# A fused decaying-attention and token-mixer kernel: first batch's v scaled on VectorE, another order of loads and constants, states from two partial sums, mixer pieces spread, tail split over two engines

## The chip, the cores and the metric

One Trainium2 chip, one of its cores. The metric is device time in microseconds of one execution. TensorE (PE in the rows, PEld its weight loads), VectorE (DVE), ScalarE (ACT), GpSimd (POOL) and SyncE (SP) each run their own queue in the order in which the program wrote it.

## What is computed

Linear attention with a decay per head over 4 batches, 8 heads, 768 positions and head width 64, and then a token mixer without a softmax on the attention's output, all given in float32:

```
# attention, head by head, in blocks of positions
intra = (q k^T * lam^(i-j), i >= j) v
inter = (q * lam^(i+1)) state
state = lam^block * state + (k * lam^(block-1-j))^T v
# mixer; x is the attention's output, heads side by side [4, 768, 512]
wq, wk = x @ w_q, x @ w_k                      # [768, 64] each
mixed  = (wq @ wk^T / 8) @ x                   # no softmax
out    = relu(mixed) @ w_out                   # [4, 768, 512]
```

## The kernel before

The work unit is a pair: one batch b and two heads, so 4 pairs per batch (kk = 0 to 3) and 16 in all (n = 0 to 15). The 768 positions are cut into six chunks of 128; the two heads of a pair sit on the two halves of the 128 partitions. The decay is folded into the operands: v is divided by a power of lam (scale_v, L169, tile vn, with the table DvI), and q is multiplied by one when it has been transposed (qT, with the tables Dq). Then the state before chunk c is a plain sum of k^T v over the chunks ahead of it.

For each pair: load casts q, k and v to bf16 by three DMAs issued from GpSimd's queue (L72, L78: fq, fk, fv); scale_v multiplies v by DvI, for pair 0 on VectorE and for all others on GpSimd; turn (L187) transposes q and k on TensorE into trq and trk, which VectorE (qT) and ScalarE (kT) bring to SBUF; states (L219) sums k^T v into the five states at once (dps), and one VectorE cast copies them out (gs, L235); scores (L238) makes k q^T and VectorE masks it in four pieces (pr, L260); inter (L264) and values (L281) add the two products into oa, which ScalarE copies to xT (L300); flip (L308) transposes xT back, and VectorE copies it to xnat.

The mixer of a batch runs inside the pairs of the next batch: mix_pq and mix_pk in kk = 0 (projections, qkT and wkn), mix_py in kk = 1 (Y), mix_pm in kk = 2 (eight products pm, each with a ReLU on ScalarE into rmT, L374), and mix_po for each of six chunks (po, copied to osb by ScalarE, L392, and stored by SyncE). The line with done (L428) says in which pair which of the six po run. The last batch's mixer is a tail behind the loop.

The order of all work is the order in which the loop writes it: there is no scheduler (manual_schedule). In turn n of the loop TensorE gets scores(n), mixer pieces, flip(n-1), inter(n), values(n), states(n+1), turn(n+2). All PSUM tiles are taken in turn from one pool of eight buffers, so a tile waits for the tile eight places earlier to be copied out. GpSimd's queue carries all loads and 15 of the 16 scalings in one line; in the loop load(n+5) stands ahead of scale_v(n+2):

```
    for n in range(N):
        if n + AHEAD < N:
            load(n + AHEAD)
        ...
        if n + 2 < N:
            scale_v(n + 2)
```

Names: trq, trk, sc, dps, oa, xp, pq, pk, py, pm and po are PSUM tiles; wqk and wo hold the mixer's weights; E48, ET, ident, maskc, swap, lnl and lncol are constants of the start.

## Time and profile before

| | us |
|---|---|
| median of 3 runs (119.08 to 119.41) | 119.2 |
| the profiled execution | 119.18 |
| its span, first to last instruction | 117.5 |
| TensorE busy | 90.8 (77%) |
| GpSimd busy | 71.0 (60%) |
| ScalarE busy | 67.6 (58%) |
| VectorE busy | 60.2 (51%) |

The sum of the prediction is made against the profiled execution, 119.18 us, of which 1.7 us lie outside the span; it stands within 0.02 us of the median. A busy share is a mean over stages that have different limits: GpSimd's work ends some 80 us into the span, the mixer starts only with the second batch, and the tail has no loads and hardly any VectorE work.

### The profile page before, as it was taken

To read this page: it belongs to the slowest core of one execution; us is meant where nothing else is said; L and a number is where in the kernel's file an instruction comes from. 1 tells how busy PE (TensorE), PEld (TensorE's weight loads), DVE (VectorE), ACT (ScalarE), POOL (GpSimd) and SP (SyncE) were. 2 spreads that over 40 slices of the span, in tenths; PEclk is the share of its full clock that TensorE was granted. 3 is DMA by queue.
4 is the path that set the end of the run, shared out by engine and by line. 5 is a ranking of instruction groups with operands and counts; after the bars stand their busy time and mean duration, and the time that the engine had idled before them with its cause. 6 is when DMAs were issued, how large, how long until landed. Compare 5 with 4: busy or idle time off the path is not lost. (4 is left out here: it accounts for less than half of the span.)

```text
span 117.5 us, 3292 instructions
## 1 busy us (share of the span) xinstructions
PE 90.8 (77%) x1380; PEld 60.1 (51%) x1392; DVE 60.2 (51%) x124; ACT 67.6 (58%) x123; POOL 71.0 (60%) x74
## 2 busy tenths in 40 slices
PE   0046992009988999799999988999999898976960
PEld 0046681008867757384858646575766463621420
DVE  1716874004896698555746892938398371110000
ACT  4409553002344638985666599585839957449750
POOL 5994799999999999999999996240000000000000
PEclk9999999555799999999999999999999999999998
DMA  1999999999999999999999999570400025140283
GB/s 29 188 210 162 143 86 147 162 157 161 163 189 165 169 160 144 160 148 192 241 231 164 267 168 165 103 268 0 179 6 0 6 89 206 62 169 15 93 310 132
DMA packets 67934, 17.06 MB, mean 145 GB/s; under 512 B 64336, under 2 KB 64848, under 8 KB 67920
## 3 DMA queue, kind: packets, MB, share of 16 engines
q0 software_dynamic: 61216, 9.77, 112.2%
q1 hardware_dynamic: 6704, 7.08, 17.9%
q8 instruction: 11, 0.18, 0.6%
q14 instruction: 3, 0.02, 0.1%
HBM read 20.32 MB, written 6.29 MB: 226 GB/s over the span
## 5 line engine op out<-in xcount | busy, mean ns | idle before, releaser
L260 DVE TENSOR_TENSOR pr<-sc,maskc 128x384 bf16<-128x384 f32 x64 | 31.2, 550 | 1.0 <-PE sc L248 1.0
L179 POOL TENSOR_TENSOR vn<-fv,DvI 128x768 bf16<-128x768 bf16 x15 | 22.6, 1510 | 7.2 <-PE oa L292 3.9
L384 PE MATMUL po<-wo,rmT 128*128 128x512 bf16 x87 | 23.0, 380 | 3.2 <-ACT rmT L374 2.8
L235 DVE CAST gs<-dps 128x320 bf16<-128x320 f32 x16 | 7.9, 492 | 30.0 <-PE dps L226 30.0
L213 ACT COPY kT<-trk 128x768 bf16<-128x768 bf16 x16 | 12.8, 798 | 16.7 <-PE trk L209 16.7
L300 ACT CAST xT<-oa 128x384 bf16<-128x384 f32 x32 | 17.2, 592 | 6.8 <-PE oa L292 6.0
L392 ACT COPY osb<-po 128x512 f32<-128x512 f32 x24 | 14.1, 585 | 9.3 <-PE po L384 7.0
L384 PEld LDWEIGHTS <-rmT 128*128 128x128 bf16 x96 | 9.0, 98 | 13.9 <-ACT rmT L374 5.9
L78 POOL DMA_DIRECT2D fv<-in_v_dram x15 | 15.7, 1049 | 0.0
L78 POOL DMA_DIRECT2D fk<-in_k_dram x15 | 15.6, 1041 | 0.0
L226 PE MATMUL dps<-vn,fk 128*64 128x320 bf16 (+4 forms) x150 | 9.2, 254 | 7.9 <-POOL vn L179 7.9
L194 PE MATMUL trq<-ident,fq 128*64 128x128 bf16 x192 | 9.3, 237 | 7.5 <-DMA fq<-in_q_dram 7.5
L72 POOL DMA_DIRECT2D fq<-in_q_dram x16 | 14.4, 898 | 0.8 <-POOLq L468 0.8
L374 ACT ACTIVATE rmT<-pm 128x384 bf16<-128x384 f32 x32 | 12.7, 530 | 0.4 <-PE pm L367 0.4
L226 PEld LDWEIGHTS <-fk 128*64 128x64 bf16 x150 | 7.9, 113 | 8.7 <-issue 8.2
L292 PE MATMUL oa<-pr,vn 128*64 128x128 bf16 x192 | 10.3, 228 | 1.1 <-DVE pr L260 0.7
L194 PEld LDWEIGHTS <-fq 128*64 128x64 bf16 x192 | 6.9, 121 | 7.5 <-DMA fq<-in_q_dram 7.5
L313 DVE COPY xnat<-xp 128x768 bf16<-128x768 bf16 x16 | 8.8, 550 | 3.5 <-PE xp L312 3.5
L312 PE MATMUL xp<-ident,xT 128*128 128x128 bf16 x96 | 8.6, 226 | 0.6 <-ACT xT L300 0.5
L200 DVE TENSOR_TENSOR qT<-trq,dq 128x768 bf16<-128x768 bf16 x16 | 8.8, 550 | 0.4 <-PE trq L194 0.4
L248 PE MATMUL sc<-qT,kT 64*128 64x128 bf16 x192 | 8.8, 229 | 0.0
L292 PEld LDWEIGHTS <-vn 128*64 128x64 bf16 x192 | 6.7, 112 | 3.7 <-issue 2.1
(45 smaller groups left out, 95.7 us busy)
## 6 DMA issues: line engine op xcount, KB each, us to landing
out_dram<-osb SPq DMA_DIRECT2D x24, 256.0 KB, 2.0
fq<-in_q_dram POOLq DMA_DIRECT2D x16, 192.0 KB, 5.9
fk<-in_k_dram POOLq DMA_DIRECT2D x15, 192.0 KB, 6.4
fv<-in_v_dram POOLq DMA_DIRECT2D x15, 192.0 KB, 6.7
wo<-in_moe_w_out_dram POOLq DMA_DIRECT2D x1, 512.0 KB, 7.3
k<-in_k_dram SPq DMA_DIRECT2D x1, 384.0 KB, 4.0
v<-in_v_dram SPq DMA_DIRECT2D x1, 384.0 KB, 7.1
wqk<-in_moe_w_q_dram POOLq DMA_DIRECT2D x2, 64.0 KB, 5.3
```

The lines of the kernel that those rows point to most:

```text
L72: nc.gpsimd.dma_start(out=t, in_=q_rows(n))
L78: nc.gpsimd.dma_start(out=t, in_=kv_rows(n, src))
L179: eng.tensor_tensor(out=vn, in0=fv, in1=DvI[:, 2 * kk : 2 * kk + 2, :].unsqueeze(3).to_broadcast([128, 2, NCH, D]), op=ALU.mult,)
L194: nc.tensor.transpose(trq[hl * 64 : hl * 64 + 64, a, r, :], fq[:, hl, a, r * D : (r + 1) * D], ident,)
L213: nc.scalar.copy(out=kT, in_=trk)
L226: nc.tensor.matmul(dps[hl * 64 : hl * 64 + 64, c:, :], kn[:, hl, c, :], vn[:, hl, c, :].unsqueeze(1).to_broadcast([128, m, D]), start=(c = ...
L260: nc.vector.tensor_tensor(out=t, in0=sc[a, hl], in1=maskc, op=ALU.mult)
L292: nc.tensor.matmul(oa[a][r, cc, :], vn[:, hl, c, :], pr[a, hl][:, cc, :], start=False, stop=(cc == 2), skip_group_check=True,)
L300: nc.scalar.copy(out=xT[b][:, kk, a * HALF : (a + 1) * HALF].rearrange("d (c p r) -> d c r p", c=3, r=2), in_=oa[a].rearrange("d c (r p) - ...
L374: nc.scalar.activation(out=M[b]["rmT"][:, dd, n * HALF : (n + 1) * HALF], in_=pm, func=ACT.Relu, scale=1.0 / 8.0,)
L384: nc.tensor.matmul(po, M[b]["rmT"][:, kt, t * CH : (t + 1) * CH], wo[:, kt, :], start=(kt == 0), stop=(kt == 3),)
L392: nc.scalar.copy(out=osb, in_=po)
```

## The change

v of pair 0 is loaded as the other v are, from GpSimd's queue in bf16 and right behind the first q, and no longer by SyncE in float32. The scalings of pairs 1 to 3 move from GpSimd to VectorE; GpSimd scales from pair 4 on. load(1), load(2), load(3) and load(4) now follow one another with only constants between them, and the three casting loads of the mixer's projection weights on GpSimd become two float32 loads on SyncE and three casts on ScalarE in the loop's second turn, together with the two copies that make swap. states multiplies chunks 0 and 1 into the first two states only, and chunks 2 to 4 into the last three; VectorE then copies the second state aside (two), casts the first two, and adds two to the last three. mix_pm is cut in halves, one behind turn in kk = 1 and one in kk = 2; three po stand in kk = 2 and three in kk = 3. Behind the loop flip stands later, one more po is there, and the tail's copies of Y, its ReLUs and its output copies alternate between ScalarE and VectorE.

```diff
     load_q(0)
+    t0 = stage.tile([128, 2, NCH, D], BF16, tag="fv", name="fv")
+    nc.gpsimd.dma_start(out=t0, in_=kv_rows(0, v))
+    staged[0, "v"] = t0
...
-    v0 = consts.tile([128, 2, NCH, D], F32, name="v0")
-    nc.sync.dma_start(out=v0, in_=kv_rows(0, v))
+    wqk_f = consts.tile([128, 2, 4, DHY], F32, name="wqk_f")
+    for i, w in enumerate((moe_w_q, moe_w_k)):
+        nc.sync.dma_start(out=wqk_f[:, i], in_=w.rearrange("(kt p) j -> p kt j", p=128))
...
-    def load_wqk():
-        for at, w in ((0, moe_w_q), (1, moe_w_k), (2, moe_w_q)):
-            nc.gpsimd.dma_start(
-                out=wqk[:, :, at * DHY : (at + 1) * DHY],
-                in_=w.rearrange("(kt p) j -> p kt j", p=128),
-            )
+    def cast_wqk():
+        nc.scalar.copy(out=wqk[:, :, 0:DHY], in_=wqk_f[:, 0])
+        nc.scalar.copy(out=wqk[:, :, DHY : 2 * DHY], in_=wqk_f[:, 1])
+        nc.scalar.copy(out=wqk[:, :, 2 * DHY :], in_=wqk_f[:, 0])
+        nc.vector.tensor_copy(out=swap[:, 0:64], in_=ident[:, 64:128])
+        nc.vector.tensor_copy(out=swap[:, 64:128], in_=ident[:, 0:64])
...
         for c in range(NCH - 1):
-            m = NCH - 1 - c
+            end = 2 if c < 2 else NCH - 1
             for hl in range(2):
                 nc.tensor.matmul(
-                    dps[hl * 64 : hl * 64 + 64, c:, :],
+                    dps[hl * 64 : hl * 64 + 64, c:end, :],
                     kn[:, hl, c, :],
-                    vn[:, hl, c, :].unsqueeze(1).to_broadcast([128, m, D]),
+                    vn[:, hl, c, :].unsqueeze(1).to_broadcast([128, end - c, D]),
...
-        nc.vector.tensor_copy(out=gs, in_=dps)
+        two = gsp.tile([128, 1, D], F32, tag="two", name="two")
+        nc.vector.tensor_copy(out=two, in_=dps[:, 1:2, :])
+        nc.vector.tensor_copy(out=gs[:, 0:2, :], in_=dps[:, 0:2, :])
+        nc.vector.tensor_tensor(
+            out=gs[:, 2:, :],
+            in0=dps[:, 2:, :],
+            in1=two.to_broadcast([128, NCH - 3, D]),
+            op=ALU.add,
+        )
...
+        if last:
+            nc.vector.tensor_copy(out=Y[:, 0:256], in_=py[:, 0:256])
+            nc.scalar.copy(out=Y[:, 256:], in_=py[:, 256:])
...
+                if last and dd % 2:
+                    nc.vector.tensor_scalar(
+                        out=to,
+                        in0=pms[dd, n],
...
+        if last and t % 2:
+            nc.vector.tensor_copy(out=osb, in_=po)
...
         if n + 2 < N:
-            scale_v(n + 2)
+            take_k(n + 2)
+            if n + 2 >= NP:
+                scale_v(n + 2, nc.gpsimd)
...
-        done = {0: [(2, 4), (2, 5)], 1: [], 2: [(1, 0)], 3: [(1, 1), (1, 2), (1, 3)]}[kk]
+        done = {0: [], 1: [], 2: [(2, 3), (2, 4), (2, 5)], 3: [(1, 0), (1, 1), (1, 2)]}[kk]
...
         inter(n)
+        if n + 2 < NP:
+            scale_v(n + 2, nc.vector)
         values(n)
...
+        if b >= 1 and kk == 1:
+            mix_pm(b - 1, (0, 1))
+        if b >= 1 and kk == 2:
+            mix_pm(b - 1, (2, 3))
     bl = B - 1
+    mix_po(bl - 1, 3)
+    mix_pq(bl)
     flip(N - 1)
-    mix_pq(bl)
     mix_po(bl - 1, 4)
     mix_pk(bl)
     mix_po(bl - 1, 5)
-    mix_py(bl)
-    for dd in range(4):
-        mix_pm(bl, dd)
+    mix_py(bl, last=True)
+    mix_pm(bl, (0, 1, 2, 3), last=True)
```

GpSimd's queue before, from the loads of pair 4 on (fq_230, fk_232, fv_234 are pair 4, the next three pair 5, fq_339 to fv_343 pair 6; vn_242 and vn_346 are the scaled v of pairs 2 and 3):

```order
L72 DMA fq_230<-in_q_dram 128x6x128
L78 DMA fk_232<-in_k_dram 128x12x64
L78 DMA fv_234<-in_v_dram 128x12x64
L72 DMA fq_236<-in_q_dram 128x6x128
L78 DMA fk_238<-in_k_dram 128x12x64
L78 DMA fv_240<-in_v_dram 128x12x64
L179 TENSOR_TENSOR vn_242<-fv_141,DvI_124 128x768
L72 DMA fq_339<-in_q_dram 128x6x128
L78 DMA fk_341<-in_k_dram 128x12x64
L78 DMA fv_343<-in_v_dram 128x12x64
L163 DMA wo_131<-in_moe_w_out_dram 128x4x512
L179 TENSOR_TENSOR vn_346<-fv_195,DvI_124 128x768
```

And after, from the weights wo on (fq_344 to fv_348 are pair 6, fq_461 to fv_465 pair 7, vn_467 and vn_579 the scaled v of pairs 4 and 5):

```order
L175 DMA wo_138<-in_moe_w_out_dram 128x4x512
L71 DMA fq_344<-in_q_dram 128x6x128
L77 DMA fk_346<-in_k_dram 128x12x64
L77 DMA fv_348<-in_v_dram 128x12x64
L71 DMA fq_461<-in_q_dram 128x6x128
L77 DMA fk_463<-in_k_dram 128x12x64
L77 DMA fv_465<-in_v_dram 128x12x64
L193 TENSOR_TENSOR vn_467<-fv_234,DvI_134 128x768
L71 DMA fq_573<-in_q_dram 128x6x128
L77 DMA fk_575<-in_k_dram 128x12x64
L77 DMA fv_577<-in_v_dram 128x12x64
L193 TENSOR_TENSOR vn_579<-fv_240,DvI_134 128x768
```

GpSimd's first scaling now stands behind the loads of pair 7, where before that of pair 2 stood behind the loads of pair 5 and that of pair 3 behind wo.

VectorE's queue before, from the states of pair 0 to the first masked scores of pair 1:

```order
L235 CAST gs_184<-dps_173 128x320
L200 TENSOR_TENSOR qT_210<-trq_197,dq1_127 128x768
L260 TENSOR_TENSOR pr_260<-sc0_244,maskc_111 128x384
L260 TENSOR_TENSOR pr_262<-sc1_245,maskc_111 128x384
L260 TENSOR_TENSOR pr_264<-sc0_252,maskc_111 128x384
L260 TENSOR_TENSOR pr_266<-sc1_253,maskc_111 128x384
L235 CAST gs_307<-dps_296 128x320
L200 TENSOR_TENSOR qT_322<-trq_309,dq2_128 128x768
L260 TENSOR_TENSOR pr_364<-sc0_348,maskc_111 128x384
```

And after, from the query of pair 1 to the query of pair 2 (vn_227 and vn_280 are the scaled v of pairs 1 and 2):

```order
L214 TENSOR_TENSOR qT_204<-trq_191,dq1_131 128x768
L193 TENSOR_TENSOR vn_227<-fv_114,DvI_134 128x768
L282 TENSOR_TENSOR pr_259<-sc0_243,maskc_101 128x384
L282 TENSOR_TENSOR pr_261<-sc1_244,maskc_101 128x384
L282 TENSOR_TENSOR pr_263<-sc0_251,maskc_101 128x384
L282 TENSOR_TENSOR pr_265<-sc1_252,maskc_101 128x384
L193 TENSOR_TENSOR vn_280<-fv_121,DvI_134 128x768
L250 COPY two_310<-dps_298 128x64
L251 CAST gs_309<-dps_298 128x128
L252 TENSOR_TENSOR gs_309<-dps_298,two_310 128x192
L214 TENSOR_TENSOR qT_327<-trq_314,dq2_132 128x768
```

The scaling of pair 1 stands ahead of pair 0's masked scores (pr), that of pair 2 ahead of pair 1's states, and the one cast of the states has become three instructions.

ScalarE's queue before, in the second batch's turn kk = 2, from the fifth of eight ReLUs to the copies of three output chunks:

```order
L374 ACTIVATE rmT_849<-pm_963 128x384
L374 ACTIVATE rmT_849<-pm_966 128x384
L374 ACTIVATE rmT_849<-pm_969 128x384
L374 ACTIVATE rmT_849<-pm_972 128x384
L392 COPY osb_988<-po_983 128x512
L300 CAST xT_732<-oa_991 128x3x2x64
L300 CAST xT_732<-oa_992 128x3x2x64
L213 COPY kT_1058<-trk_1045 128x768
L392 COPY osb_1105<-po_1100 128x512
L392 COPY osb_1113<-po_1108 128x512
L392 COPY osb_1121<-po_1116 128x512
```

And after, from the last ReLU of the first half to the output copies of the next turn:

```order
L416 ACTIVATE rmT_870<-pm_949 128x384
L322 CAST xT_750<-oa_995 128x3x2x64
L322 CAST xT_750<-oa_996 128x3x2x64
L227 COPY kT_1065<-trk_1052 128x768
L416 ACTIVATE rmT_870<-pm_1067 128x384
L416 ACTIVATE rmT_870<-pm_1071 128x384
L416 ACTIVATE rmT_870<-pm_1069 128x384
L416 ACTIVATE rmT_870<-pm_1073 128x384
L434 COPY osb_1124<-po_1119 128x512
L434 COPY osb_1132<-po_1127 128x512
L434 COPY osb_1140<-po_1135 128x512
```

Four ReLUs now stand behind the copy of kT at a turn's end, where eight stood in a row ahead of the next turn's output copy.

## Rows read from the trace of the kernel before

**Rows 1.** The page's 40 slices: busy tenths of TensorE.

```profile
PE   0046992009988999799999988999999898976960
```

**Rows 2.** Timeline (start, length, engine, line, operation; idle before), 19 to 27 us.

```profile
19.07 0.89 POOL L72 DMA_DIRECT2D fq<-in_q_dram  x1
...
21.89 0.91 POOL L72 DMA_DIRECT2D fq<-in_q_dram  x1
...
24.72 1.59 POOL L179 TENSOR_TENSOR vn<-fv,DvI 128x768 bf16<-128x768 bf16 x1
...
26.37 1.01 PE L226 MATMUL dps<-vn,fk 128*64 128x320 bf16 x10 [7.57 <-POOL vn L179]
```

**Rows 3.** Windows: us; busy PE, PEld, DVE, ACT, POOL; granted clock; DMA share, GB/s.

```profile
26.40:31.10 4.70, 4.70 (x69) 3.92 (x69) 3.02 (x7) 0.80 (x1) 4.70 (x5) 0.50 2.28 165
...
31.10:36.90 5.80, 5.04 (x118) 4.03 (x114) 4.36 (x10) 3.02 (x5) 5.80 (x7) 1.00 1.75 177
```

**Rows 4.** DMA issues (KB, us to landing): q of pairs 4 and 5.

```profile
fq<-in_q_dram POOLq DMA_DIRECT2D x1, 192.0 KB, 5.0
...
fq<-in_q_dram POOLq DMA_DIRECT2D x1, 192.0 KB, 5.8
```

**Rows 5.** Timeline of the first 15 us.

```profile
3.21 0.82 POOL L107 IOTA ET<- 128x768 f32 x1
...
3.29 0.78 DVE L127 COPY swap<-ident 128x64 bf16<-128x64 bf16 x1 [1.96 <-POOL ident masks.py:199]
...
8.91 0.96 DVE L179 TENSOR_TENSOR vn<-v,DvI 128x768 bf16<-128x768 f32 x1 [2.64 <-DMA v<-in_v_dram]
...
12.56 1.47 POOL L179 TENSOR_TENSOR vn<-fv,DvI 128x768 bf16<-128x768 bf16 x1 [2.31 <-DMA fv<-in_v_dram]
...
12.74 1.95 DVE L260 TENSOR_TENSOR pr<-sc,maskc 128x384 bf16<-128x384 f32 x4 [0.51 <-PE sc L248]
```

**Rows 6.** Timeline of VectorE in pair 3, and pair 4's scores.

```profile
32.05 0.49 DVE L235 CAST gs<-dps 128x320 bf16<-128x320 f32 x1 [0.51 <-PE dps L226]
...
32.46 0.55 DVE L200 TENSOR_TENSOR qT<-trq,dq 128x768 bf16<-128x768 bf16 x1
...
32.99 1.95 DVE L260 TENSOR_TENSOR pr<-sc,maskc 128x384 bf16<-128x384 f32 x4
...
36.91 0.51 PE L248 MATMUL sc<-qT,kT 64*128 64x128 bf16 x12
```

**Rows 7.** Timeline of TensorE in pair 9 (kk = 1).

```profile
63.45 0.51 PE L248 MATMUL sc<-qT,kT 64*128 64x128 bf16 x12
...
66.38 0.58 PE L226 MATMUL dps<-vn,fk 128*64 128x320 bf16 x10
...
66.79 0.51 PE L194 MATMUL trq<-ident,fq 128*64 128x128 bf16 x12
...
67.56 0.51 PE L248 MATMUL sc<-qT,kT 64*128 64x128 bf16 x12
```

**Rows 8.** Timeline: scores of pairs 8, 11, 12; ScalarE's ReLUs in pair 10.

```profile
57.16 0.51 PE L248 MATMUL sc<-qT,kT 64*128 64x128 bf16 x12
...
68.36 3.18 ACT L374 ACTIVATE rmT<-pm 128x384 bf16<-128x384 f32 x8
...
73.48 0.51 PE L248 MATMUL sc<-qT,kT 64*128 64x128 bf16 x12
...
78.89 0.51 PE L248 MATMUL sc<-qT,kT 64*128 64x128 bf16 x12
```

**Rows 9.** Timeline of the tail.

```profile
99.46 0.79 PE L312 MATMUL xp<-ident,xT 128*128 128x128 bf16 x6 [0.51 <-ACT xT L300]
...
105.59 0.82 PE L367 MATMUL pm<-qkT,Y 64*128 64x384 bf16 x8 [0.68 <-ACT Y L359]
...
105.96 3.17 ACT L374 ACTIVATE rmT<-pm 128x384 bf16<-128x384 f32 x8 [0.43 <-PE pm L367]
...
108.81 4.71 PE L384 MATMUL po<-wo,rmT 128*128 128x512 bf16 x21 [0.38 <-ACT rmT L374]
```

More of the change, by code (lines that the diff above doesn't have):

```diff
@@ L8 @@
 from concourse._compat import with_exitstack
-from concourse.masks import make_identity
 BF16 = mybir.dt.bfloat16
@@ L90 @@
     nc.sync.dma_start(out=k0, in_=kv_rows(0, k))
[L91 to L92 removed]
+    wqk_f = consts.tile([128, 2, 4, DHY], F32, name="wqk_f")
+    for i, w in enumerate((moe_w_q, moe_w_k)):
+        nc.sync.dma_start(out=wqk_f[:, i], in_=w.rearrange("(kt p) j -> p kt j", p=128))
     nc.scalar.preload_act_table_set("natural_log_exp_and_others")
+    ident = consts.tile([128, 128], BF16, name="ident")
+    nc.vector.memset(ident, 0.0)
+    maskc = consts.tile([128, 3, CH], BF16, name="maskc")
+    nc.vector.memset(maskc, 1.0)
+    nc.gpsimd.affine_select(
+        out=ident,
+        in_=ident,
+        compare_op=ALU.not_equal,
+        fill=1.0,
+        base=0,
+        pattern=[[-1, 128]],
+        channel_multiplier=1,
+    )
     E48 = consts.tile([128, H, NCH], F32, name="E48")
@@ L125 @@
     )
-    swap = consts.tile([128, 128], BF16, name="swap")
-    nc.vector.tensor_copy(out=swap[:, 0:64], in_=ident[:, 64:128])
-    nc.vector.tensor_copy(out=swap[:, 64:128], in_=ident[:, 0:64])
+    load(2)
     lnl = consts.tile([128, H], F32, name="lnl")
     nc.scalar.activation(out=lnl, in_=lam_all, func=ACT.Ln)
+    lnv = lnl.rearrange("p (k l) -> p k l", l=2)
+    lncol = consts.tile([128, NP], F32, name="lncol")
+    for hl in range(2):
+        nc.vector.tensor_copy(
+            out=lncol[hl * 64 : hl * 64 + 64, :], in_=lnv[hl * 64 : hl * 64 + 64, :, hl]
+        )
     pw48 = consts.tile([128, H, NCH], F32, name="pw48")
@@ L137 @@
     )
-    lnv = lnl.rearrange("p (k l) -> p k l", l=2)
-    lncol = consts.tile([128, NP], F32, name="lncol")
-    for hl in range(2):
-        nc.vector.tensor_copy(
-            out=lncol[hl * 64 : hl * 64 + 64, :], in_=lnv[hl * 64 : hl * 64 + 64, :, hl]
-        )
-    DvI = consts.tile([128, H, NCH], F32, name="DvI")
-    nc.scalar.activation(out=DvI, in_=pw48, func=ACT.Exp, scale=-1.0)
     Dq = [consts.tile([128, S], BF16, name=f"dq{kk}") for kk in range(NP)]
@@ L346, in mix_pk, with mix_py @@
         M[b]["wkn"] = wkn
-    def mix_py(b):
+    def mix_py(b, last=False):
         py = pst([128, HD], F32, "py")
@@ L391, in mix_po @@
         osb = outp.tile([128, HD], F32, tag="osb", name="osb")
-        nc.scalar.copy(out=osb, in_=po)
+        if last and t % 2:
+            nc.vector.tensor_copy(out=osb, in_=po)
+        else:
+            nc.scalar.copy(out=osb, in_=po)
         nc.sync.dma_start(out=out[b, t * CH : (t + 1) * CH, :], in_=osb)
     make_dq(0)
-    scale_v(0)
-    load(2)
+    take_k(0)
     turn(0)
+    scale_v(0, nc.vector)
     states(0)
     make_dq(1)
+    take_k(1)
+    turn(1)
+    load(3)
+    scale_v(1, nc.vector)
     make_dq(2)
-    make_dq(3)
-    scale_v(1)
-    load(3)
-    turn(1)
-    load_wqk()
     load(4)
@@ L448 @@
     mix_po(bl - 1, 5)
-    mix_py(bl)
-    for dd in range(4):
-        mix_pm(bl, dd)
+    mix_py(bl, last=True)
+    mix_pm(bl, (0, 1, 2, 3), last=True)
     for t in range(NCH):
-        mix_po(bl, t)
+        mix_po(bl, t, last=True)
 _INS = ['q', 'k', 'v', 'lam', 'moe_w_q', 'moe_w_k', 'moe_w_out']
```

80 lines of the change are left out of this document (46 added, 34 removed).

## The prediction

> **What bounds the kernel now.** I read the page's slices first, then the timeline, and the waits where TensorE stands still. The 40 slices of TensorE show three stretches [rows 1]: work with holes in the first third, a nearly solid middle, and a thinning tail. In the hole TensorE waits 7.57 us for v of pair 2 [rows 2]. VectorE and ScalarE are empty there too; only GpSimd works, at loads, because the scaling of pair 2 stands in its queue behind the loads of pairs 3 to 5. So the first batch is paced by GpSimd's order, and when TensorE comes back its granted clock is 0.50, the 1.2 GHz level, for 4.7 us; from 31.1 us on it is 1.00 [rows 3]. The middle is paced by TensorE: pair 9 runs from its scores to the next scores in 67.56 - 63.45 = 4.11 us [rows 7] with its matmuls in one unbroken row. The exception is kk = 2: pair 10 takes 5.92 us, beside eight ReLUs that hold ScalarE for 3.18 us [rows 7, 8]. In the tail TensorE waits for ScalarE at three places [rows 9].
>
> **First batch, the large term.** The new order takes the scalings of pairs 1 to 3 off GpSimd, so the wait of 7.57 us has nothing left to wait for. What is late next? Two things: the transfers and VectorE.
>
> The transfers: loads of pairs 4 and 5 were issued 2.82 us apart [rows 2] but q landed at 19.07 + 5.0 = 24.07 and 21.89 + 5.8 = 27.69 us, 3.62 us apart [rows 4]. So a pair's three loads take 3.6 us to come in, however fast GpSimd issues them (0.94 us each, 2.82 / 3). v of pair 1 was in at 12.56 us [rows 5]. v of pair 0 now stands ahead of it in the same queue, one load more, less a short memset that leaves: I put it at 13.2, and v of pair 2 at 16.8. Removing the float32 load of v from SyncE may give some of that back; the projection weights, now on SyncE, take some.
>
> VectorE in the new order, step by step. v of pair 1 at 13.2, scaled in 0.96 us. That duration is from the float32 v of pair 0 on VectorE [rows 5]; with v in bf16 the nearest other row is qT with 0.55 [rows 6], whose operands are all 16 bits wide while DvI is not, so I keep 0.96. The masked scores of pair 0, queued behind it, begin at 14.15 and not at 12.74, and take 1.95 [rows 5]: 16.1. Scaling of pair 2 waits for its v until 16.8: 17.75. Then the states, three instructions for one. One of 320 columns takes 0.49, a masking of 384 takes 0.55, and four maskings 1.95 [rows 5, 6]: about 0.94 ns a column and 0.19 us fixed, of which 0.08 overlaps with the one ahead. That makes 0.36 + 3 x 0.19 - 2 x 0.08 = 0.77, and I take 0.75: 18.5. qT of pair 2, 0.5: 19.0. Pair 1: masking 1.95, the two swap copies, xnat 0.55 (the size of qT), scaling of pair 3 0.96, states 0.75, qT 0.5. The swap copies ran for 0.78 and 0.71 us, one on top of the other, until GpSimd's table ET was written [rows 5]; since GpSimd will be issuing loads here too I take 0.8 for both. Sum 5.5: pair 2's masking at 24.5. Pairs 2 and 3 have 1.95 + 0.55 + 0.75 + 0.5 = 3.75 and a turnaround on TensorE of some 0.05: pair 3's masking from 28.3 to 30.25. TensorE then has the last values of pair 3, the states and the transposes of the next pairs (1.18 us from states to scores in pair 9 [rows 7], less 0.16 by the shorter states): scores of pair 4 at 31.4 us. Before they began at 36.91 [rows 6]. **Gain 5.5 us.**
>
> By the Trainium skill (SBUF — State Buffer, section Who interferes with whom) a VectorE copy in a two-port mode and a GpSimd instruction shut each other out for a whole instruction. The trace agrees: both swap copies ended within 0.1 us of ET. If each copy waited out one load, 1.9 us in place of 0.8, the forecast below would be 110.4.
>
> Bounds: the states between 0.49 (one cast) and 1.47 (three), the scaling between 0.55 and 1.51 (GpSimd's 1.47 to 1.59), the swap copies between 0.4 (64 columns each by the rate above) and 1.9 (a whole load each). Together the gain lies between 2 and 7.
>
> What is hidden: GpSimd's first scaling, of pair 4, stands behind the loads of pairs 5 to 7. From the loads of pair 1 at 4.7 us (ET ended at 4.03 [rows 5], plus the 0.7 of one load more), seven times 2.82, a mask and wo end near 26, and the scaling at 27.5; TensorE wants it at 30.4. That cover is 3 us; without it each microsecond is one of the result. Afterwards GpSimd needs 2.82 + 1.5 = 4.3 us a pair, about as much as the loop. The three casts of the weights and the Dq table that moved into the loop lie on ScalarE, which had 2.8 of 5.8 us free in pairs 3 and 4 [rows 3]; at ScalarE's 0.40 us a ReLU of 384 columns they are at most 1.2 us. If that cover were gone they would cost as much. SyncE has nothing queued before the first output.
>
> **The loop, pairs 4 to 15.** Two sums of 576 columns for one of 960: states last 66.79 - 66.38 = 0.41 us on TensorE [rows 7], so 0.25 after, 0.16 a pair, 0.65 a batch. Spreading the mixer: a po is four of the 21 matmuls that take 4.71 us, 0.9, py 1.35 by the same rate, eight pm 0.82 [rows 9]. Packed, pair 10 would be pair 9 without py but with one po and eight pm, 4.11 - 1.35 + 0.9 + 0.82 = 4.48; it took 5.92, so 1.44 us a batch is stall behind ReLUs. Not all of it goes. After the change four ReLUs stand behind the copy of kT, in two turns. TensorE's next scores need buffers that kT's copy and then the first ReLU release: I count about 0.6 us for each turn, 1.2 a batch, so 0.25 is won. The longer states chain delays the masking in kk = 0 and 1, where two po no longer cover it: 0.1 lost. Together 0.8 a batch, and a batch of 78.89 - 57.16 = 21.73 us [rows 8] comes to 20.9. For three batches **2.4 us**; bounds are 0 (all stalls stay) and 5 (all go). One po leaves the loop for the tail, which cancels.
>
> **The tail.** The eight ReLUs run on ScalarE alone, and between the first and TensorE's unbroken run lie 108.81 - 105.96 = 2.85 us [rows 9]. On two engines, four each at 0.40 and about 0.5, the first half is ready after some 1.4: 1.45 won. Halving Y shortens a wait of 0.68 by 0.2, and the wait of 0.51 for xT is covered by the po put there [rows 9]; the last output copy on VectorE costs 0.1. **2.0 us**, between 1 and 3.
>
> **Sum.** 119.18 - 5.5 - 2.4 - 2.0 = **109.3 us**, from the profiled execution, which lies on the median; its own range is 107 to 111.5.
>
> **Rivals.**
> First, VectorE becomes the bound of the first batch at its dear end: three states instructions at 1.47 us cost 0.72 more in each of four pairs, 2.9 in all, 112.2 us. For it speaks that VectorE has no free place in that walk; against it that four maskings overlap in the trace.
> Second, the spread mixer wins nothing: ReLUs behind kT hold back the next scores as long as eight together did. The loop's gain falls to 0, 111.7. For it: kT's copy already stands at the end of a turn. Against it: no turn has to wait for more than four.
> Third, the change doesn't take GpSimd off the pace: its issues are held to the rate at which transfers come in. Five pairs' loads at 3.62 for 2.82 put the scaling of pair 4 4.0 us later, 0.9 past its need, and with a pace of 4.3 the delay is carried for some pairs: about 110.6. Against it: GpSimd issued six loads in 5.65 us without a pause [rows 2].
> Fourth, slower than before: TensorE's clock. In the new first batch TensorE waits a while in every pair; if its grant stays at the lower level into the solid middle, states take 1.01 for 0.58 [rows 2, 7], 1.74 times, and a packed pair 3.0 us more. From the fourth such pair on the gain of 9.9 is eaten; five pairs give 124. Against it: it came back to 1.00 after 4.7 us of work, and held it through pair 3 with its waits [rows 3].
>
> **How the numbers follow.** This kernel's measurement can tell about 0.3% from no change. Forecast 0.62, first rival 0.14, second 0.12, third 0.08, fourth 0.03, and 0.01 that losses of these kinds cancel the gain. So faster 0.96, same 0.01, slower 0.03. The range takes in the forecast's bounds and the first three rivals: 106 to 113.
>
> **What would show it.** No wait of TensorE over 2 us between 10 us and the end; VectorE solid in pairs 0 to 3, with states of three instructions in 0.75 us; scores of pair 4 near 31.4; batches of 20.9; two stalls of 0.6 in place of one of 1.4; the tail's first po complete 1.4 us after the first ReLU. A first batch that ends later than 33.5, a granted clock of 0.50 past 30 us, or a scaling on GpSimd that TensorE waits for would make it wrong.

## The result and the profile after

The changed kernel takes **109.41 us** (median; 109.25 to 109.8), the one before 119.16: a ratio of 0.9183, with a 95% interval of 0.9155 to 0.9211. The forecast was 109.3. Its profiled execution took 109.8 us with a span of 108.0, against 119.18 and 117.5 before, so the two spans differ by 9.5 us. The total was hit; the three terms were not, and their misses nearly cancel. The rest of this document is about that. Two slow executions are left out of the ratios, one of the kernel before (120.84 us) and one of s_best (120.97 us, at a mean granted clock of 0.788).

First the page's slices, for [rows 1]: TensorE's busy tenths, its granted clock, and the share of the DMA engines.

```profile
PE   0013979977796998899999999999999999998950
...
PEclk9999999999999999999999999999999999999999
DMA  0999999999999999999999999990000435522383
```

The empty slices between 18 and 26 us are filled and the tail thins less; the first 10 us are emptier than before. The DMA row will matter below: for the first 70 us, all slices but the first show the 16 engines busy for 90% or more. The view of waits of TensorE (us in total, times, longest) says what is left:

```profile
PE dps L240 <- DVE vn L193: 1.7, 1, 1.7
PE dps L240 <- POOL vn L193: 1.6, 3, 0.9
```

The wait of 7.57 us for GpSimd's scaling [rows 2] has become three, 1.6 us together. The other, 1.7 us, is for VectorE's scaling of pair 0 (9.84 to 10.80 us), which waits for its load; that wait was there before, with 0.9 us. The timeline of the first batch (start, length, engine, line, operation; idle before) answers to [rows 5, 6] and is the walk of the prediction:

```profile
13.39 0.96 DVE L193 TENSOR_TENSOR vn<-fv,DvI 128x768 bf16<-128x768 bf16 x1 [0.55 <-DMA fv<-in_v_dram]
14.27 1.95 DVE L282 TENSOR_TENSOR pr<-sc,maskc 128x384 bf16<-128x384 f32 x4
17.00 0.96 DVE L193 TENSOR_TENSOR vn<-fv,DvI 128x768 bf16<-128x768 bf16 x1 [0.79 <-DMA fv<-in_v_dram]
17.88 0.22 DVE L250 COPY two<-dps 128x64 f32<-128x64 f32 x1
18.01 0.28 DVE L251 CAST gs<-dps 128x128 bf16<-128x128 f32 x1
18.21 0.35 DVE L252 TENSOR_TENSOR gs<-dps,two 128x192 bf16<-128x192 f32 x1
18.47 0.55 DVE L214 TENSOR_TENSOR qT<-trq,dq 128x768 bf16<-128x768 bf16 x1
18.97 1.95 DVE L282 TENSOR_TENSOR pr<-sc,maskc 128x384 bf16<-128x384 f32 x4
20.84 0.17 DVE L171 COPY swap<-ident 128x64 bf16<-128x64 bf16 x1
20.92 0.18 DVE L172 COPY swap<-ident 128x64 bf16<-128x64 bf16 x1
...
23.39 1.95 DVE L282 TENSOR_TENSOR pr<-sc,maskc 128x384 bf16<-128x384 f32 x4
...
27.09 1.94 DVE L282 TENSOR_TENSOR pr<-sc,maskc 128x384 bf16<-128x384 f32 x4
```

The masking of pairs 0 to 3 was forecast at 14.15, 19.0, 24.5 and 28.3. The first two stand where they were put; then the swap copies and the states take less than was thought. TensorE's states of pair 4, its scores, and the states of pair 5:

```profile
29.84 0.42 PE L240 MATMUL dps<-vn,fk 128*64 128x128 bf16 x9 [0.44 <-POOL vn L193]
...
30.89 0.51 PE L270 MATMUL sc<-qT,kT 64*128 64x128 bf16 x12
...
34.87 0.42 PE L240 MATMUL dps<-vn,fk 128*64 128x128 bf16 x9 [0.87 <-POOL vn L193]
```

Pair 4's scores begin at 30.89 and not 36.91 [rows 6]: 6.0 us won, 31.4 forecast. The two waits on GpSimd are new. The loop (timeline of TensorE, pairs 8 to 11) answers to [rows 7, 8]:

```profile
51.11 0.51 PE L270 MATMUL sc<-qT,kT 64*128 64x128 bf16 x12
51.55 0.51 PE L334 MATMUL xp<-ident,xT 128*128 128x128 bf16 x6
...
59.81 0.52 PE L270 MATMUL sc<-qT,kT 64*128 64x128 bf16 x7
...
60.88 0.49 PE L334 MATMUL xp<-ident,xT 128*128 128x128 bf16 x6
...
66.06 0.95 PE L270 MATMUL sc<-qT,kT 64*128 64x128 bf16 x12
67.08 0.49 PE L334 MATMUL xp<-ident,xT 128*128 128x128 bf16 x6
...
71.92 0.45 PE L270 MATMUL sc<-qT,kT 64*128 64x128 bf16 x10
```

A free pair goes from scores to xp in 51.55 - 51.11 = 0.44 us; pairs 10 and 11 take 1.07 and 1.02, so each stalls 0.6 us. That is one stall of 1.44 turned into two of 0.6, as forecast. This batch takes 71.92 - 51.11 = 20.81 us against 21.73 [rows 8]. The tail, for [rows 9]:

```profile
97.23 0.42 DVE L382 CAST Y<-py 128x256 bf16<-128x256 f32 x1 [1.67 <-PE py L373]
97.69 0.37 ACT L383 CAST Y<-py 128x256 bf16<-128x256 f32 x1 [1.19 <-DVE Y L382]
97.71 0.90 PE L395 MATMUL pm<-qkT,Y 64*128 64x384 bf16 x8 [0.59 <-DVE Y L382]
98.08 1.66 ACT L416 ACTIVATE rmT<-pm 128x384 bf16<-128x384 f32 x4
98.31 1.95 DVE L407 TENSOR_SCALAR rmT<-pm 128x384 bf16<-128x384 f32 x4 [0.66 <-PE pm L395]
98.62 5.47 PE L423 MATMUL po<-wo,rmT 128*128 128x512 bf16 x24
```

Between the first ReLU and TensorE's unbroken run now lie 0.54 us, 2.85 before. To the end of that run, which holds more of the po now, it is 104.09 - 98.08 = 6.01 us for 113.52 - 105.96 = 7.56: 1.55 us won. But the two halves of Y run one after the other: ScalarE starts when VectorE has ended.

Put together by stretches of the two spans: to pair 4's scores 6.0 us won; pairs 4 to 7 take 51.11 - 30.89 = 20.22 against 57.16 - 36.91 = 20.25, nothing; pairs 8 to 11 0.92; the rest 36.08 (from 71.92 to 108.0) against 38.61 (from 78.89 to 117.5), 2.5. One po of 0.9 us has moved from pairs 4 to 7 to the end, which hides in these numbers: like for like, pairs 4 to 7 **lost** 0.9 us and the end won 3.4. The question is therefore what held pairs 4 to 7.

### The profile page after: what moved, and what is told of

Read it like the earlier page. It is cut to its first block, busy times and chain, and to the rows that moved or that the text cites. A ratio compares the mean times of both kernels' runs of the same rounds, so it can differ in the third digit from the quotient of the medians.

```text
span 108.0 us, 3286 instructions
## 1 busy us (share of the span) xinstructions
PE 88.6 (82%) x1392; PEld 58.7 (54%) x1392; DVE 69.3 (64%) x168; ACT 65.2 (60%) x119; POOL 65.5 (61%) x68
## 5 line engine op out<-in xcount | busy, mean ns | idle before, releaser
L423 PE MATMUL po<-wo,rmT 128*128 128x512 bf16 x96 | 22.3, 379 | 0.0
L193 POOL TENSOR_TENSOR vn<-fv,DvI 128x768 bf16<-128x768 bf16 x12 | 17.8, 1498 | 3.8 <-PE trk L223 3.8
L434 ACT COPY osb<-po 128x512 f32<-128x512 f32 x21 | 12.3, 586 | 8.8 <-PE po L423 7.2
L250 DVE COPY two<-dps 128x64 f32<-128x64 f32 x16 | 3.6, 224 | 16.6 <-PE dps L240 16.6
L314 PE MATMUL oa<-pr,vn 128*64 128x128 bf16 x192 | 10.9, 228 | 2.6 <-DVE pr L282 2.2
L270 PE MATMUL sc<-qT,kT 64*128 64x128 bf16 x192 | 10.8, 228 | 0.9 <-ACT kT L227 0.5
L416 ACT ACTIVATE rmT<-pm 128x384 bf16<-128x384 f32 x28 | 11.5, 507 | 0.0
L270 PEld LDWEIGHTS <-kT 64*128 64x128 bf16 x192 | 7.1, 99 | 4.2 <-issue 2.1
L223 PE MATMUL trk<-ident,fk 128*64 128x128 bf16 x180 | 8.4, 232 | 0.1
```

Source lines behind the costliest of these rows:

```text
L193: eng.tensor_tensor(out=vn, in0=fv, in1=DvI[:, 2 * kk : 2 * kk + 2, :].unsqueeze(3).to_broadcast([128, 2, NCH, D]), op=ALU.mult,)
L270: nc.tensor.matmul(sc[a, hl][:, cc, :], kT[r, c * CH : (c + 1) * CH], qchunk(n, r, c), start=True, stop=True, skip_group_check=True,)
L314: nc.tensor.matmul(oa[a][r, cc, :], vn[:, hl, c, :], pr[a, hl][:, cc, :], start=False, stop=(cc == 2), skip_group_check=True,)
L416: nc.scalar.activation(out=to, in_=pms[dd, n], func=ACT.Relu, scale=1.0 / 8.0)
L423: nc.tensor.matmul(po, M[b]["rmT"][:, kt, t * CH : (t + 1) * CH], wo[:, kt, :], start=(kt == 0), stop=(kt == 3),)
L434: nc.scalar.copy(out=osb, in_=po)
```

## Experiments: parts of the change by themselves

All times are medians, ratios are against the kernel before on the same chip, with 95% intervals. The chips differ: the kernel before took 119.16 to 119.46 us on them, so a difference between medians from two chips means little below some 0.3 us, and rows are set beside it. Parts of the change are taken back one by one first.

**Scaling of pairs 1 to 3 back on GpSimd** (u_scale_gpsimd), all else as changed.

```diff
-    scale_v(1, nc.vector)
+    scale_v(1, nc.gpsimd)
...
-            scale_v(n + 2, nc.vector)
+            scale_v(n + 2, nc.gpsimd)
```

> The changed kernel with one part undone: v of pairs 1 to 3 scaled on GpSimd, at the same places of the program, all else as after the change (109.4 us). My theory: the hole of the first batch came from the scalings standing in GpSimd's queue behind loads, so it comes back; but the loads now follow one another earlier, so pair 2's scaled v comes near 22 us instead of 26.3 and pair 3's near 27, and the scores of pair 4 begin near 33.6 instead of 30.9: 112 us. Rival (the order of loads and constants is what helped, the engine of the scaling is not): 109.4. Rival (the order of loads is worth nothing): the whole hole is back, scores of pair 4 near 36.5, 115 us.

Measured: 111.41 us, ratio 0.9328 (0.9311 to 0.9346). The view of waits of TensorE:

```profile
PE dps L240 <- POOL vn L193: 4.1, 3, 3.7
```

The wait for GpSimd is back at half its size (3.7 us), and pair 4's scores begin at 33.21, as the theory had it. So of the 6.0 us of the first batch 2.3 belong to the engine of the scaling, and the other 3.7 to the rest of the change; that the order of loads and constants makes up most of them is argued, since no run took it back alone. In time 2.0 us are lost.

**One sum for the states** (u_one_sum): the five blocks summed in one piece of TensorE's work and cast once.

```diff
-            end = 2 if c < 2 else NCH - 1
+            m = NCH - 1 - c
...
-                    dps[hl * 64 : hl * 64 + 64, c:end, :],
+                    dps[hl * 64 : hl * 64 + 64, c:, :],
...
-                    vn[:, hl, c, :].unsqueeze(1).to_broadcast([128, end - c, D]),
+                    vn[:, hl, c, :].unsqueeze(1).to_broadcast([128, m, D]),
...
-        nc.vector.tensor_copy(out=two, in_=dps[:, 1:2, :])
-        nc.vector.tensor_copy(out=gs[:, 0:2, :], in_=dps[:, 0:2, :])
-        nc.vector.tensor_tensor(
-            out=gs[:, 2:, :],
-            in0=dps[:, 2:, :],
-            in1=two.to_broadcast([128, NCH - 3, D]),
-            op=ALU.add,
-        )
+        nc.vector.tensor_copy(out=gs, in_=dps)
```

> The changed kernel with the states as one sum and one cast, as before, all else as after. Theory: TensorE paces batches 2 and 3 and loses 0.16 us in each of their eight pairs, 1.3 us; in the first batch, paced by VectorE, the single cast is 0.1 us shorter in each of four pairs, 0.4 won back; the second batch waits for GpSimd anyhow: 110.3 us. Rival, VectorE paces everywhere: 0.1 us won in 16 pairs, 107.8. Rival, neither: 109.4.

Measured: 110.43 us (110.22 to 111.41), ratio 0.9262 (0.9218 to 0.9307): the two sums are worth 1.0 us, in spite of two more instructions on VectorE in each pair.

**Mixer in the loop and head of the tail as before** (u_mixer_old).

```diff
-        done = {0: [], 1: [], 2: [(2, 3), (2, 4), (2, 5)], 3: [(1, 0), (1, 1), (1, 2)]}[kk]
+        done = {0: [(2, 4), (2, 5)], 1: [], 2: [(1, 0)], 3: [(1, 1), (1, 2), (1, 3)]}[kk]
...
+        if b >= 1 and kk == 2:
+            for dd in range(4):
+                mix_pm(b - 1, (dd,))
...
-        if b >= 1 and kk == 1:
-            mix_pm(b - 1, (0, 1))
-        if b >= 1 and kk == 2:
-            mix_pm(b - 1, (2, 3))
...
-    mix_po(bl - 1, 3)
-    mix_pq(bl)
     flip(N - 1)
+    mix_pq(bl)
```

> The changed kernel with the mixer's pieces in the loop and the head of the tail back at their places of before (all eight pm and their ReLUs in kk = 2, the po as before, flip ahead of pq), all else as after. Prediction's theory: spreading wins 0.25 us a batch of the 1.44 us of stall, loses 0.1 in kk = 0 and 1, and the order at the tail's head wins 0.5: 110.3 us. Rival A, most of the stall is won by the spreading: pair 10 takes 1.4 us longer again in every batch, 112.5. Rival B, spreading moves the stall only: 109.9, by the tail's head alone.

Measured: 110.79 us, ratio 0.9276 (0.9255 to 0.9297): spread and head are worth 1.4 us. TensorE's waits for the ReLUs are back (1.3 us in four), and so is the one for xT (0.5). Where the 1.4 lie: pairs 8 to 11 take 72.41 - 51.31 = 21.10 us for 20.81, so the spread wins 0.3 in a full batch (0.25 forecast); from pair 12 to the end 36.59 for 36.08, with one po of 0.9 less there, so 1.4 like for like. Split at the last values of pair 15 (91.63 and 90.64), 19.22 for 18.72 lie ahead, so the spread wins 0.5 in the last batch, and the head of the tail the other 0.9.

**The tail on ScalarE alone** (u_tail_scalar): Y, the ReLUs and the output copies without VectorE, in the changed order.

```diff
-    mix_py(bl, last=True)
-    mix_pm(bl, (0, 1, 2, 3), last=True)
+    mix_py(bl)
+    mix_pm(bl, (0, 1, 2, 3))
...
-        mix_po(bl, t, last=True)
+        mix_po(bl, t)
```

> The changed kernel with the tail's copies and ReLUs on ScalarE alone, as before; the tail's order stays as after. Theory: between the first of the last eight ReLUs and an unbroken run of output matmuls lie 2.85 us again, so 1.5 us are lost, Y in two halves is worth 0.15, the last copy on ScalarE wins 0.1: 110.9 us. Rival, the tail is bound by its output matmuls and stores and the split changes nothing: 109.4.

Measured: 109.95 us, ratio 0.9208 (0.918 to 0.9237). Only 0.5 us is lost, and the theory fell. Timeline of this tail:

```profile
97.82 3.17 ACT L416 ACTIVATE rmT<-pm 128x384 bf16<-128x384 f32 x8 [0.42 <-PE pm L395]
98.37 5.85 PE L423 MATMUL po<-wo,rmT 128*128 128x512 bf16 x23
```

ScalarE's eight ReLUs last as long as before [rows 9], and yet TensorE starts on po 0.55 us after their beginning. What has changed is which come first: the left half of S of all four blocks, which is all that the first three po read.

**The ReLUs turned back** (t_relu_old): the same, and the eight ReLUs in the old order. This was run to test the new explanation.

```diff
-    mix_pm(bl, (0, 1, 2, 3))
+    for dd in range(4):
+        mix_pm(bl, (dd,))
```

> The changed kernel with its tail on ScalarE alone (as in the run on the tail) and, on top, the eight last ReLUs in the order of the kernel before: block by block, both halves of S of a block one after the other, instead of the first half of all four blocks first. The same instructions on the same engine, only turned round. Theory: the order won the ReLU term. The first po needs the first half of all four blocks, that is the seventh ReLU in place of the fourth, so three ReLUs of 0.40 us later: 109.95 + 1.2 = 111.15 us, and the first unbroken row of po begins some 2.8 us after the first ReLU, as in the kernel before. Rival: the order is worth nothing, since the po of later rows wait all the same: 109.95 within 0.3. Rival: the second engine did win most of it and the run on the tail hid its loss elsewhere: also near 110.

Measured: 110.83 us, ratio 0.9295 (0.9262 to 0.9328). The timeline:

```profile
98.11 3.17 ACT L416 ACTIVATE rmT<-pm 128x384 bf16<-128x384 f32 x8 [0.42 <-PE pm L395]
...
100.95 4.71 PE L423 MATMUL po<-wo,rmT 128*128 128x512 bf16 x21 [0.38 <-ACT rmT L416]
```

The old picture is back: 100.95 - 98.11 = 2.84 us, as in [rows 9]. So the order is worth 110.83 - 109.95 = 0.9 us and the second engine 0.5. The rows bear it out: from the first ReLU to the end of the unbroken run it is 6.01 us in the changed kernel, 6.40 on ScalarE alone and 7.55 with the old order. Together they are the 1.45 us of the prediction; the reason given for it there was the smaller half.

## Experiments: what held pairs 4 to 7

GpSimd's timeline in the changed kernel has waits that it did not have before:

```profile
23.27 1.01 POOL L77 DMA_DIRECT2D fk<-in_k_dram  x1 [1.57 <-DMA fq<-in_q_dram]
...
28.30 1.49 POOL L193 TENSOR_TENSOR vn<-fv,DvI 128x768 bf16<-128x768 bf16 x1
...
31.29 1.01 POOL L77 DMA_DIRECT2D fk<-in_k_dram  x1 [0.69 <-DMA wo<-in_moe_w_out_dram]
...
33.33 1.49 POOL L193 TENSOR_TENSOR vn<-fv,DvI 128x768 bf16<-128x768 bf16 x1
```

Loads wait for loads. In all four such holds of this trace the load that is waited for stands eight places earlier in GpSimd's queue: q of pair 4 for k of pair 6, wo for k of pair 8, and two shorter ones. In the trace of before no load waits for another: there GpSimd, held up by its own scalings, seems not to have come eight ahead of the transfers. Now it does: the scaling of pair 4 starts at 28.30, behind the loads of pairs 6 and 7, of which those of pair 6 were held for 1.9 us. It ends at 29.8; forecast were 27.5, and TensorE's need came at 29.4 in place of 30.4.

**Scaling ahead of the loads** (m_scale_first): in each turn of the loop GpSimd scales v before it issues the loads of five pairs on. Theory: the queue's order is the cause. Rival: GpSimd's own work of 4.3 us a pair is.

```diff
-        if n + AHEAD < N:
-            load(n + AHEAD)
-        if n == 0:
-            load_wo()
         if n + 2 < N:
             take_k(n + 2)
             if n + 2 >= NP:
                 scale_v(n + 2, nc.gpsimd)
+        if n + AHEAD < N:
+            load(n + AHEAD)
+        if n == 0:
+            load_wo()
```

> The changed kernel with one line of the loop moved: GpSimd's scaling of pair n+2 stands ahead of the loads of pair n+5 in its queue, not behind them. Theory: in the second batch TensorE waits 0.44, 0.87 and 0.26 us for scalings on GpSimd, because loads ahead of them are held until the load eight places earlier has landed; with the scaling ahead these waits go and the loads are early enough: 1.4 us won, 108.0 us. Rival, the waits only cover others (VectorE's masking or the transfers) or come back as waits for q and k: 109.4.

Measured: **107.56 us** (107.28 to 108.24), ratio 0.9009 (0.8973 to 0.9046). GpSimd's timeline:

```profile
23.51 1.01 POOL L77 DMA_DIRECT2D fk<-in_k_dram  x1 [1.96 <-DMA fq<-in_q_dram]
...
25.53 1.49 POOL L193 TENSOR_TENSOR vn<-fv,DvI 128x768 bf16<-128x768 bf16 x1
...
29.86 1.50 POOL L193 TENSOR_TENSOR vn<-fv,DvI 128x768 bf16<-128x768 bf16 x1
```

GpSimd's first loads are still held (1.96 us at k of pair 6, 1.57 in the changed kernel), but the scalings stand ahead of the next ones and come 2.8 and 3.5 us earlier. No wait of TensorE for GpSimd's scaling is left. The timeline of TensorE has the scores of pairs 4 and 8:

```profile
30.13 0.51 PE L270 MATMUL sc<-qT,kT 64*128 64x128 bf16 x12
...
48.63 0.51 PE L270 MATMUL sc<-qT,kT 64*128 64x128 bf16 x12
```

Pairs 4 to 7 take 48.63 - 30.13 = 18.50 us, 1.7 less than in the changed kernel, and 1.75 less than before. Of that 0.9 is the moved po, and 0.85 is what the prediction had for a batch (0.8). The wait ahead of pair 4's scores goes too: from pair 3's scores to pair 8's it is 48.63 - 26.45 = 22.18 us for 51.11 - 26.58 = 24.53 (24.28 and 24.80 in the two runs that change only the tail).

**The packed mixer on top of that** (s_mixer_old): is the 1.7 us the spread's, which only needed GpSimd out of its way, or GpSimd's alone? The edit is that of u_mixer_old, on m_scale_first.

> The kernel with GpSimd's scaling ahead of its loads (107.56 us), with the mixer's pieces in the loop and the head of the tail put back to the places of the kernel before. Theory: in the changed kernel pairs 4 to 7 ran at GpSimd's pace, so the spread of the mixer could win nothing there; with that pace gone it wins there too. In the changed kernel the spread and the head of the tail were worth 1.4 us, in two batches and the tail; with the first batch's mixer in pairs 4 to 7 added I expect 0.6 to 0.9 more, 2.0 to 2.3 in all: 109.6 to 109.9 us, and pairs 4 to 7 19.2 to 19.6 us instead of 18.5. Rival: the spread wins only what it won before, 1.4, and the 1.7 us that pairs 4 to 7 gave back was GpSimd's pace alone: 109.0. Rival: the packed mixer gives GpSimd time and the two gains overlap: 108.3.

Measured: 108.92 us, ratio 0.9128 (0.9099 to 0.9157), 1.36 above m_scale_first. That is the same 1.4 as without the earlier scaling. Pairs 4 to 7 take 49.43 - 30.01 = 19.42 us, as the theory had it, but the whole 0.92 above m_scale_first is the one po more that stands in them. So the theory's reason fell and the first rival holds: the spread wins nothing in pairs 4 to 7, and in the later ones what it won before (0.3 in pairs 8 to 11 and 0.5 in 12 to 15, by the same rows); the 1.7 us were GpSimd's order alone.

**wo by SyncE** (m_wo_sync): the output weights as float32 by SyncE, cast by ScalarE in pairs 4 and 5; one load fewer in GpSimd's queue.

```diff
-        nc.gpsimd.dma_start(out=wo, in_=moe_w_out.rearrange("(kt p) j -> p kt j", p=128))
+        nc.vector.memset(wo_f[:, 0, 0:1], 0.0)
+        nc.sync.dma_start(out=wo_f, in_=moe_w_out.rearrange("(kt p) j -> p kt j", p=128))
...
-        if n == 0:
-            load_wo()
...
             cast_wqk()
+            load_wo()
+        if n in (4, 5):
+            cast_wo((2 * n - 8, 2 * n - 7))
```

> The changed kernel with the output weights wo loaded by SyncE as float32, after the swap copies, and cast by ScalarE in four copies of 128x512 in pairs 4 and 5: one load of the 22 ahead of the third scaling leaves GpSimd's queue. In the changed kernel GpSimd spent 1.15 us from the issue of wo to the next load, was held 0.69 us later on by the landing of wo, and the scaling of pair 4 and pair 5 were waited for by TensorE for 0.44 and 0.87 us, a later one for 0.26. Theory (GpSimd's queue, held to its loads, paces pairs 4 to 7): the scalings come 1.2 to 1.9 us earlier, those waits go, 1.2 to 1.6 us are won, less some 0.3 for ScalarE's casts of 0.6 each beside kT and xT: 108.1 to 108.5 us. Rival: the transfers themselves are the pace, and wo takes its time on the same 16 engines from whichever queue: the holds stay, 109.2 to 109.6. Rival: the casts delay kT and xT by their whole 2.4 us in pairs 4 and 5: 110 or more.

Measured: 109.91 us (109.79 to 110.25), ratio 0.9214 (0.9194 to 0.9234): 0.5 above the changed kernel, at the edge of what can be told, and between the two rivals. GpSimd's timeline:

```profile
27.01 1.49 POOL L200 TENSOR_TENSOR vn<-fv,DvI 128x768 bf16<-128x768 bf16 x1
...
30.49 0.88 POOL L71 DMA_DIRECT2D fq<-in_q_dram  x1 [2.00 <-DMA fk<-in_k_dram]
...
33.92 1.49 POOL L200 TENSOR_TENSOR vn<-fv,DvI 128x768 bf16<-128x768 bf16 x1
```

The first scaling came 1.3 us earlier, and the next hold, 2.0 us, gave it back: pair 5's scaling is 0.6 later than in the changed kernel, with one wait of 1.7 us on TensorE. That fits the first rival: wo takes its share of the 16 engines from whichever queue it comes, the holds are the pace of the transfers, and GpSimd's queue only hands them on. The run doesn't settle it, since wo as float32 also brings 1024 KB to SBUF where 512 were brought before, and how much of the 0.5 ScalarE's casts add, it doesn't tell either.

**v of the first pair by SyncE** (u_v0_sync): as float32, as in the kernel before; the load in GpSimd's queue taken out.

```diff
-    t0 = stage.tile([128, 2, NCH, D], BF16, tag="fv", name="fv")
-    nc.gpsimd.dma_start(out=t0, in_=kv_rows(0, v))
-    staged[0, "v"] = t0
...
+    v0 = consts.tile([128, 2, NCH, D], F32, name="v0")
+    nc.sync.dma_start(out=v0, in_=kv_rows(0, v))
+    staged[0, "v"] = v0
```

> The changed kernel with v of pair 0 loaded by SyncE in float32 again, as before; scaled on VectorE as in both. Theory: the first batch is paced by transfers up to the masking of pair 0 (14.3 us). One load less stands ahead of v of pair 1 in GpSimd's queue, so it lands 0.9 us earlier and the masked scores of pair 0 begin near 13.5; v of pairs 2 and 3 move along: 0.7 us won, 108.7. Rival, the same bytes are only fetched from another queue and share the same time: 109.4. Rival, v of pair 0 itself comes later beside k and the weights on SyncE: slower, 110.

Measured: 110.18 us (109.52 to 110.67), ratio 0.9216 (0.9175 to 0.9258): nothing won, perhaps some tenths lost. The timeline of VectorE in the first pairs:

```profile
13.85 0.96 DVE L193 TENSOR_TENSOR vn<-fv,DvI 128x768 bf16<-128x768 bf16 x1 [1.75 <-DMA fv<-in_v_dram]
```

v of pair 1 comes 0.46 us **later** than in the changed kernel, though one load fewer stands ahead of it (in the runs that leave the start as it is, it is scaled at 13.01 to 13.39). It is the same finding at another place, with the same reserve: a load moved to another queue is still a load, and this one brings 384 KB as float32 for 192. No run moved a load at the same size.

## Experiments: the start and a better tail

**42 idle transposes before the first work** (m_warm): in the changed kernel TensorE's first transposes of 12 take 0.85 us, the later ones 0.53.

```diff
+    warm = pst([128, S], BF16, "warm")
+    for i in range(42):
+        c = i % NCH
+        nc.tensor.transpose(warm[:, c * CH : (c + 1) * CH], ident, ident)
     turn(0)
```

> The changed kernel with 42 more transposes of the identity matrix on TensorE ahead of its first work, written to a PSUM tile that nobody reads, some 3 us of work between 4 and 7.5 us. After the change twelve transposes take 0.85 to 0.88 us until 17 us and 0.53 from 21 us on, while before they took 0.53 from 15.3 us on. Theory: with work ahead the faster rate is there from pair 0 on, but this stretch is paced by transfers and VectorE, so at most 0.4 us are won: 109.0. Rival, TensorE's slow start paces the first batch: 1.5 us won, 107.9. Rival, the extra work delays the first transposes: 110.

Measured: 109.41 us, ratio 0.9166 (0.9131 to 0.9202): nothing won. The timeline:

```profile
7.95 0.53 PE L208 MATMUL trq<-ident,fq 128*64 128x128 bf16 x12
...
18.16 0.82 PE L270 MATMUL sc<-qT,kT 64*128 64x128 bf16 x12
```

The first transposes are fast now, and pair 0's scores start at 12.36 for 13.03 (12.54 to 12.89 in most other runs, so little of it is sure). But by pair 1 TensorE has waited again and is slow again, and this time the page's clock row shows it, in slices of 2.7 us:

```profile
PEclk9999965599999999999999999999999999999998
```

In the window from 16 to 20 us the grant is 0.50, which the changed kernel doesn't have. VectorE's masking of pair 0 stands behind the scaling of pair 1 in any case, whose v comes hardly earlier (scaled at 13.12 for 13.39). So the run doesn't tell what a fast start alone would win.

**py as two tiles** (s_two_y), on m_scale_first: in the program ScalarE's half of Y waits for VectorE's, since both read one tile of py. Here the first half of py is copied while TensorE makes the second.

```diff
-        py = pst([128, HD], F32, "py")
...
+        for i in range(w):
+            py = pst([128, half], F32, "py")
...
+            if i == 0 and last:
+                nc.vector.tensor_copy(out=M[b]["Yh"][0], in_=py)
+            else:
+                nc.scalar.copy(out=M[b]["Y"][:, i * half :], in_=py)
...
```

> The kernel with GpSimd's scaling ahead of its loads (107.56 us), and in the tail py as two tiles of 256 columns, each with its own six matmuls, VectorE copying the first while TensorE makes the second, ScalarE the second. In the changed kernel both copies read one tile, ScalarE's waited for VectorE's, and TensorE for 0.59 us. Theory: the first copy lies beside the second half of py, and the second beside the first four pm, so the wait goes but for some 0.1, less 0.1 for six more matmuls: 0.4 us won, 107.15 us. Rival: the wait moves to the second half (ScalarE's copy of 0.37 and the turnaround stand in front of the fifth pm): 0.2 or nothing, 107.4 to 107.6.

Measured: **106.55 us** (106.33 to 107.45), ratio 0.8916 (0.8888 to 0.8944). The timeline of TensorE:

```profile
93.93 1.47 PE L378 MATMUL py<-xnat,wkn 128*128 128x256 bf16 x12
...
95.34 1.03 PE L397 MATMUL pm<-qkT,Y 64*128 64x384 bf16 x8
```

From the first py to the first pm 1.41 us, against 95.22 - 93.18 = 2.04 in m_scale_first: 0.6 won. The medians differ by 1.0; the other 0.4 stands in no row. Both together, **py as two tiles and wo by SyncE** (s_best):

> The kernel with GpSimd's scaling ahead of its loads and py as two tiles (106.55 us), with wo by SyncE and cast by ScalarE as above. TensorE waits for no scaling in it any more. Theory (GpSimd's pace was the one thing that the load of wo cost): nothing to win here, and up to 0.5 lost by the casts: 106.5 to 107.0 us. Rival: the landing times themselves (wo between the loads of pairs 4 and 5) still hold the first pairs: 105.8 to 106.2.

Measured: 106.72 us, ratio 0.895 (0.8926 to 0.8973), the same as s_two_y within the measurement, as expected: with the scalings ahead of the loads, a load fewer in the queue has nothing to win. Here GpSimd's scaling of pair 5 waits 2.2 us for its own v to land (it starts at 31.11, in m_scale_first at 29.86 without a wait), so the transfers came later and not earlier; TensorE didn't have to wait for it. The better version is s_two_y, 2.9 us under the changed kernel.

## Why the prediction was right, and where only by luck

| step | forecast | measured | |
|---|---|---|---|
| first batch (scores of pair 4) | 5.5 | 6.0 | swap copies and states cheaper |
| loop, three batches, like for like | 2.4 | 0.8 | -0.9, 0.9 and 0.8: GpSimd held pairs 4 to 7 |
| tail, less the po moved there | 2.0 | 2.6 | ReLUs as forecast, head 0.9 for 0.5 |
| sum | 9.9 | 9.4 | |

Against the profiled execution (119.18 - 109.8 = 9.4) the sum misses by 0.5; that execution is 0.4 above the median. For the table the end's 3.4 is split at the last values of pair 15 (98.42 before, 90.64 after): 0.8 ahead of it, 2.6 behind. Three sums of the prediction are off without harm: 30.25 + 1.18 - 0.16 is 31.3 and not 31.4; 27.5 + 4.0 lies 1.1 past the need at 30.4 and not 0.9; and the dear ends of its terms together (2.9 for the states, 1.1 for the swap copies, 0.55 for each of two scalings) would leave 0.4 of the first batch's 5.5 and not 2.

**First batch.** Right in its mechanism, its order and nearly every start. The transfers set pairs 0 to 2: v of pair 1 was scaled at 13.39 (13.2 forecast), v of pair 2 at 17.00 (16.8). VectorE set the rest, up to the wait of 0.44 us for GpSimd ahead of pair 4's scores. Mis-sized were two terms. The swap copies held the queue from 20.84 to 21.00, 0.16 us for 0.8: the slow copies of before [rows 5] did not return, although GpSimd was issuing a load from 20.87 on. The states took 18.47 - 17.88 = 0.59 for 0.75: the three instructions are 0.22 + 0.28 + 0.35 = 0.85 long where 0.36 + 3 x 0.19 = 0.93 was reckoned, and three overlaps of 0.09 come off, not two of 0.08. By the Trainium skill (SBUF — State Buffer, section Who interferes with whom) a swap copy that begins behind a GpSimd instruction could have waited it out; the trace has 0.18 us for the second, which begins 0.05 us behind that load's issue, and doesn't show it here.

**VectorE's dear end (first rival)** is out: three instructions cost 0.59, not 1.47, and u_one_sum shows that the two sums win 1.0 us in all, VectorE's part included.

**The loop.** For a batch that TensorE paces the step was right: 0.92 won in pairs 8 to 11 and 0.8 in 12 to 15 (0.8 forecast), 54.30 - 54.05 = 0.25 us from the states' matmuls to the transposes behind them, two stalls of 0.6 in the place of one of 1.44. The second rival, that spreading wins nothing, is out, though it wins only 0.3 to 0.5 a batch by u_mixer_old. The step that failed is the cover of GpSimd, "seven times 2.82" for the loads ahead of its first scaling and 3 us to spare. It counted GpSimd's issues at their own pace. They go at that of the transfers once GpSimd is eight loads ahead: 1.9 us of holds stand in front of the scaling of pair 4, which ended 0.4 us too late instead of 2.9 early. The prediction had this as its **third rival** with a chance of 0.08, and priced it at 1.3 us; by the medians m_scale_first prices it at 1.85, by the rows from pair 3's scores to pair 8's at 2.35. A scaling on GpSimd that TensorE waits for was also one of the prediction's own signs of being wrong, and it came, three times. So the rival's mechanism came true beside the forecast's, and the total was hit all the same by luck, since the first batch and the tail gave 1.1 more than their terms.

**The tail.** The ReLUs' size was right, the reason half wrong. The 1.45 us were put down to two engines; t_relu_old and u_tail_scalar show 0.9 for the order of the ReLUs and 0.5 for the second engine. Halving Y shortened TensorE's wait from 0.68 to 0.59, and not by 0.2, because the halves were queued one behind the other; s_two_y took the wait away and won 0.6. The head, where one po covers the wait for xT, was mis-sized the other way: 0.9 (u_mixer_old) for 0.5, perhaps since pq ahead of the flip fills the place as well; no run took that apart.

**The clock (fourth rival)** did not come: a mean grant of 1.000, with a 9 in all slices after. The 4.7 us at the lower level that the kernel before showed [rows 3] are gone along with the wait ahead of them; in u_scale_gpsimd, with its wait of 3.7 us, the grant is 0.50 again from 22 to 28 us.

## What to carry to other kernels

A queue that issues loads and also does work hands the transfers' pace on to that work: put the work that somebody waits for ahead of the loads that nobody needs yet, and cost the issues at the pace at which transfers land once the queue runs ahead of them (eight loads here). In two runs with the DMA row at 9, moving a load to another queue, at twice the size, won nothing. Where several results are needed before a consumer can start, look first at their order and only then for a second engine, and split a tile where two engines are to read it at once.
